# A fused RetNet attention and maxout FFN: plain first products for the first token tile, weight sums made one tile later

## The chip, the cores and the metric

The kernel runs on one core of one Trainium2 chip. The metric is the device time of one execution in microseconds (us). Five engines work side by side, each through its own instructions in order: TensorE (PE; the loading of its stationary operand is listed as PEld), VectorE (DVE), ScalarE (ACT), GpSimd (POOL), and SyncE (SP), whose queue issues nearly all transfers here.

## The reference

Causal attention with a decay (RetNet, parallel form) over 8 batches and 8 heads, then a feed-forward network that takes the maximum of three products:

```python
# q, k, v: (8, 8, 576, 64); w1, w2, w3: (512, 768); w_out: (768, 512)
scores = scale * np.matmul(q, k.transpose(0, 1, 3, 2))
gamma = 1.0 - 2.0 ** (-5.0 - np.arange(H, dtype=np.float32))
Dmat = np.where(rel >= 0, gamma[:, None, None] ** rel[None, :, :], 0.0)
attn = np.matmul(scores * Dmat[None], v).astype(np.float32)
x = attn.transpose(0, 2, 1, 3).reshape(B * S, H * D)          # (4608, 512)
h = np.maximum(np.maximum(x @ w1, x @ w2), x @ w3)
out = (h @ w_out).astype(np.float32)                          # (4608, 512)
```

The four weight matrices come as 64-bit floats and are brought to 32 bits in the kernel. All arithmetic is in 32-bit floats.

## The kernel before

The 4608 token rows are cut into 36 chunks of 128 rows (g) and 9 tiles of 512 rows (t), four chunks to a tile. Two things go on side by side: the attention of tile t + 1 and the FFN of tile t.

**Attention** of a chunk has three steps. `transposes` (L136) turns the decayed keys (`kd`, made on POOL in `decay_keys`, L130) and the queries on PE, and copies them out, kT on DVE and qT on ACT. `scores` (L149) makes the masked score block st and the running state (DVE L158, L169 or L171, POOL L172). `values` (L176) makes the output o and writes it to xT (L192); behind the last chunk of a tile DVE and POOL also make four sums of quarter blocks of xT (S, L197 to L200).

**The FFN** of a tile (`ffn`, L345) has nine units: a pair of 128-column blocks of the hidden layer (fp = 0, 1, 2) times one of the three weight matrices (i). A unit (`up`, L284) uses Strassen's scheme in Winograd's form: seven products of half-size blocks (two matmuls of 256 columns each, L293) in place of eight. It needs the S sums of xT and four sums of the weight quarters (L266, L267 on DVE; L269, L270 on POOL). Products are copied out by ACT (L298, L330) or added and compared on DVE (L311 to L333). Then four output blocks (`down`, L336) take six matmuls of 512 columns each, in one group per block (L339). In the trace each matmul of 32-bit floats shows as two instructions, so a count of x12 means six matmuls.

**Weights** come in 24 pieces of 128 x 512 (18 for the first products, 6 for the output), 512 KB each, with three buffers. `conversion` (L233) makes 32-bit floats of a piece from the two halves of its 64-bit words: `expo` and `frac` masks on DVE (L241, L246), three ACT passes (L242, L244, L248), `mant` on DVE (L249), the sign by ACT (L253), and two products on POOL, by the exponent (L254) and by the sign (L257). When both pieces of a pair are there, the four weight sums follow. The temporaries have two buffers.

**The order** is the order of the code. `convert(n)` puts n steps of the running conversion into the queues at that place. Attention's three steps alternate with units of the FFN (L388 to L397), and before, each of a unit's seven products was followed by `convert(2)` (L350), so conversions of later pieces stand in the queues of DVE, ACT and POOL between the evictions of earlier units.

## Time and profile before

| what | value |
|---|---|
| median of 3 runs | 928.27 us (927.96 to 930.12) |
| the profiled execution | 927.27 us, span 925.2 us |
| PE busy | 872.6 us (94%) |
| DVE, ACT, POOL busy | 387.5, 205.1, 177.8 us |
| granted clock of PE, mean | 0.989 |
| first matmul of the first unit, tile 0 | 43.91 us |
| first output block, tile 0 | 157.31 us |
| end of tile 0 | 183.08 us |
| tile 1 | 92.4 us |

"Busy" is the time in which an engine had at least one instruction running, and includes what an instruction waits once it has started. In a line of the trace the names are the program's with buffer numbers left out, out<-in; in square brackets stands the idle time before it and what ended it.

### The profile page before, as it was taken

The page shows a single profiled execution, that of the slowest core. Times are in us where ns is not written, and L with a number is a line of the kernel's source. Part 1 is how long each engine was busy: PE and PEld are TensorE (multiplying, and loading weights), DVE is VectorE, ACT ScalarE, POOL GpSimd, SP SyncE. Part 2 cuts the span into 40 slices and gives each one's busy share as a digit, 9 for nine tenths or more (in the row PEclk, how much of TensorE's full clock was granted, in tenths as well). Part 3 has the DMA queues.
Part 4 walks back from the last instruction along what each step waited for, and adds up shares of the span by engine and source line. Part 5 has one row for each costly group of instructions (what it writes and reads, how often), then busy time and mean ns, then how long its engine had stood idle before and what let it go on. Part 6 is the DMA issues. An engine that isn't in the chain of part 4 may idle for free.

```text
span 925.2 us, 11657 instructions
## 1 busy us (share of the span) xinstructions
PE 872.6 (94%) x4652; PEld 661.3 (71%) x4652; DVE 387.5 (42%) x692; ACT 205.1 (22%) x439; POOL 177.8 (19%) x154
## 2 busy tenths in 40 slices
PE   6676768999999999999999999999999999999998
PEld 5555555588758885888578857886788668866883
DVE  4887788244423442344334432433244334432330
ACT  2365555112111111211111111111111111111111
POOL 3767766110011001100111011100200020001000
PEclk9899999999999999999999999999999999999999
DMA  9525232150006000600060006000600050000001
GB/s 228 137 92 148 91 109 74 49 134 1 1 35 148 1 1 35 148 1 1 30 154 1 1 24 148 12 1 23 145 15 1 12 130 8 1 12 35 1 0 46
DMA packets 128550, 51.62 MB, mean 56 GB/s; under 512 B 113648, under 2 KB 122864, under 8 KB 128496
## 3 DMA queue, kind: packets, MB, share of 16 engines
q1 hardware_dynamic: 128064, 50.34, 20.6%
q8 instruction: 37, 0.61, 0.3%
q10 hardware_dynamic: 432, 0.53, 0.2%
q14 instruction: 17, 0.14, 0.0%
HBM read 41.42 MB, written 9.44 MB: 55 GB/s over the span
## 4 chain that ended last, share of the span: by engine, by line
PE 86%; DVE 7%; POOL 3%; ACT 2%; issue 1%; DMA 1%; SPq 0%; DVEq 0%; POOLq 0%; ACTq 0%
PE x L293 28%; PE down L339 20%; PE z L293 14%; PE y L293 7%; PE s L155 4%; PE o L185 3%; PE kv L166 3%; PE o L190 3%; PE kt L141 2%; DVE expo L241 2%; PE qt L141 2%; DVE mant L249 2%; POOL w L257 1%; POOL mant L254 1%; DVE frac L246 1%
## 5 line engine op out<-in xcount | busy, mean ns | idle before, releaser
L339 PE MATMUL down<-wout,h 128*128 128x512 f32 x432 | 189.9, 593 | 0.0
L293 PE MATMUL x<-S,T 128*128 128x256 f32 x648 | 169.3, 384 | 14.9 <-ACT u L298 9.3
L293 PEld LDWEIGHTS x<-S,T 128*128 128x128 f32 x648 | 123.0, 191 | 36.2 <-ACT u L298 12.4
L339 PEld LDWEIGHTS down<-wout,h 128*128 128x128 f32 x432 | 80.2, 190 | 91.8 <-issue 91.3
L172 POOL TENSOR_TENSOR state<-state,gs 128x512 f32<-128x512 f32 x24 | 31.1, 1296 | 388.4 <-DVE state L171 297.8
L293 PE MATMUL x<-S,w 128*128 128x256 f32 x324 | 85.6, 387 | 9.8 <-DVE h L321 7.2
L293 PE MATMUL z<-xT,T 128*128 128x256 f32 x324 | 84.6, 384 | 6.2 <-ACT p L298 5.8
L293 PE MATMUL z<-S,w 128*128 128x256 f32 x324 | 84.9, 385 | 0.0
L293 PE MATMUL x<-xT,w 128*128 128x256 f32 x324 | 84.9, 385 | 0.0
L293 PE MATMUL y<-xT,w 128*128 128x256 f32 x324 | 83.1, 379 | 0.0
L158 DVE TENSOR_TENSOR st<-s,causal 128x512 f32<-128x512 f32 x72 | 46.3, 685 | 78.7 <-PE s L155 78.7
L293 PEld LDWEIGHTS x<-S,w 128*128 128x128 f32 x324 | 56.5, 192 | 26.6 <-DVE h L321 5.1
L293 PEld LDWEIGHTS z<-xT,T 128*128 128x128 f32 x324 | 61.4, 191 | 16.8 <-POOL T L270 3.5
L298 ACT COPY p<-x 128x256 f32<-128x256 f32 x81 | 30.1, 371 | 187.2 <-PE x L293 187.2
L293 PEld LDWEIGHTS z<-S,w 128*128 128x128 f32 x324 | 62.7, 194 | 8.8
L293 PEld LDWEIGHTS y<-xT,w 128*128 128x128 f32 x324 | 61.6, 190 | 8.4
L321 DVE TENSOR_TENSOR tmp<-x,p 128x256 f32<-128x256 f32 x54 | 22.9, 424 | 104.8 <-PE x L293 104.1
L342 ACT COPY osb<-down 128x512 f32<-128x512 f32 x36 | 21.1, 585 | 200.1 <-PE down L339 200.1
L293 PEld LDWEIGHTS x<-xT,w 128*128 128x128 f32 x324 | 56.5, 192 | 6.3 <-issue 0.8
L130 POOL TENSOR_TENSOR kd<-kraw,gk 128x512 f32<-128x512 f32 x36 | 39.1, 1092 | 99.8 <-DMA kraw<-in_k_dram 84.8
L192 DVE TENSOR_TENSOR xT<-o,gq 128x512 f32<-128x512 f32 x36 | 24.8, 690 | 71.4 <-PE o L190 65.4
L298 ACT COPY u<-x 128x256 f32<-128x256 f32 x81 | 30.0, 370 | 100.8 <-PE x L293 99.4
(58 smaller groups left out, 924.8 us busy)
## 6 DMA issues: line engine op xcount, KB each, us to landing
bits<-in_moe_w_dram SPq DMA_DIRECT2D x18, 512.0 KB, 3.6
out_dram<-osb SPq DMA_DIRECT2D x36, 256.0 KB, 2.0
kraw<-in_k_dram SPq DMA_DIRECT2D x32, 256.0 KB, 4.0
qraw<-in_q_dram SPq DMA_DIRECT2D x32, 256.0 KB, 4.1
vraw<-in_v_dram SPq DMA_DIRECT2D x32, 256.0 KB, 4.1
bits<-in_moe_w_out_dram SPq DMA_DIRECT2D x6, 512.0 KB, 3.2
kraw<-in_k_dram SPq DMA_DIRECT2D x8, 128.0 KB, 3.5
qraw<-in_q_dram SPq DMA_DIRECT2D x8, 128.0 KB, 3.2
```

What stands on the lines that cost most here:

```text
L130: nc.gpsimd.tensor_tensor(t[:], raws.pop(("k", g))[:], gk[:].unsqueeze(2).to_broadcast([C, H, D]), op=ALU.mult)
L141: nc.tensor.transpose(pt[:, p, :], pair(src, p), ident[:C, :C])
L155: nc.tensor.matmul(s[j][:, p, :], lhsT=kT[r, p, :], rhs=qT[r, p, :], start=True, stop=True)
L158: nc.vector.tensor_tensor(st[:, j], s[j][:], masks[start_of(g)][:].unsqueeze(1).to_broadcast([C, NP, C]), op=ALU.mult)
L166: nc.tensor.matmul(kv[:, p, :], lhsT=pair(kd, p)[r:], rhs=pair(raws["v", g], p)[r:], start=True, stop=True)
L172: nc.gpsimd.tensor_tensor(t[:], t[:], gs[:], op=ALU.mult)
L185: nc.tensor.matmul(o[D * j:D * (j + 1), p, :], lhsT=vr[:, 2 * p + j, :], rhs=st[:, j, p, :], start=(p == 0), stop=(old == 0 and p == NP - ...
L190: nc.tensor.matmul(o[:, p, :old], lhsT=sd[:, p, :], rhs=qT[:, p, :old], start=False, stop=(p == NP - 1), skip_group_check=True)
L192: nc.vector.tensor_tensor(xT[t][:, :, i * C:(i + 1) * C], o[:], gq[:], op=ALU.mult)
L293: nc.tensor.matmul(out[:], lhsT=w[:, d * P:(d + 1) * P], rhs=xS[t][n][:, d, :], start=first and d == 0, stop=d == 1, skip_group_check=True)
L298: nc.scalar.copy(c[:], src[:])
L339: nc.tensor.matmul(ps[:], lhsT=h[:, fb, m * P:(m + 1) * P], rhs=w_sb["out", fb][:], start=(fb == 0), stop=(fb == NF - 1))
```

## The change

For tile 0 the first products are plain (`up_plain`): each of the 18 pieces gives one block of h by four matmuls of 512 columns into a whole PSUM bank of 512 columns; for matrix 0 ACT copies it to h, for matrices 1 and 2 DVE takes the maximum of h and it. Tile 0 so needs neither the S sums nor the weight sums. The weight sums are made by `weight_sums(n)`: the first two behind the third and fourth output block of tile 0, the others behind the units of tile 1, two units ahead of their use.

In the conversion the sign is no longer a factor. DVE takes the sign bit of the high word and puts it into the exponent factor (`bitwise_and`, then `bitwise_or`), and POOL multiplies once. A piece has four steps instead of five, and eight instructions instead of nine behind the load.

At the start the first weight piece is loaded behind chunk 2 and the second and third behind chunk 3; the key products and the first conversions stand at other places in the order.

```diff
--- before.py
+++ after.py
@@ -190,7 +190,7 @@
                 nc.tensor.matmul(o[:, p, :old], lhsT=sd[:, p, :], rhs=qT[:, p, :old],
                                  start=False, stop=(p == NP - 1), skip_group_check=True)
         nc.vector.tensor_tensor(xT[t][:, :, i * C:(i + 1) * C], o[:], gq[:], op=ALU.mult)
-        if i == CPT - 1:
+        if i == CPT - 1 and t > 0:
             x = xT[t]
             a11, a12, a21, a22 = (x[:, 2 * d:2 * d + 2, NH * r:NH * (r + 1)] for r in range(2) for d in range(2))
             s1, s2, s3, s4 = (spool.tile([P, 2, NH], FP32, tag=f"S{n}", name=f"S{n}") for n in (1, 2, 3, 4))
@@ -249,27 +249,26 @@
         nc.vector.scalar_tensor_tensor(out=mant[:], in0=frac[:], scalar=2.0 ** -20, in1=mant[:],
                                        op0=ALU.mult, op1=ALU.add)
         yield
-        sign = wtmp.tile([P, DM], FP32, tag="sign", name="sign")
-        nc.scalar.activation(sign[:], high, AF.Sign)
-        nc.gpsimd.tensor_tensor(mant[:], mant[:], expo[:].bitcast(FP32), op=ALU.mult)
-        yield
+        nc.vector.scalar_tensor_tensor(out=expo[:], in0=high, scalar=-2 ** 31, in1=expo[:],
+                                       op0=ALU.bitwise_and, op1=ALU.bitwise_or)
         w = w_sb[piece] = const.tile([P, DM], FP32, name=f"w{i}_{fb}")
-        nc.gpsimd.tensor_tensor(w[:], mant[:], sign[:], op=ALU.mult)
+        nc.gpsimd.tensor_tensor(w[:], mant[:], expo[:].bitcast(FP32), op=ALU.mult)
         load_weights(1)
         yield
-        if i == "out" or fb % 2 == 0:
+
+    def weight_sums(n):
+        if n >= len(units):
             return
+        fp, i = units[n]
         half = [slice(0, DM // 2), slice(DM // 2, DM)]
-        b11, b21 = (w_sb[i, fb - 1][:, r] for r in half)
-        b12, b22 = (w_sb[i, fb][:, r] for r in half)
-        t1, t2, t4 = (const.tile([P, DM // 2], FP32, name=f"T{n}_{i}_{fb}")[:] for n in (1, 2, 4))
+        b11, b21 = (w_sb[i, 2 * fp][:, r] for r in half)
+        b12, b22 = (w_sb[i, 2 * fp + 1][:, r] for r in half)
+        t1, t2, t4 = (const.tile([P, DM // 2], FP32, name=f"T{m}_{i}_{fp}")[:] for m in (1, 2, 4))
         nc.vector.tensor_tensor(t1, b12, b11, op=ALU.subtract)
         nc.vector.tensor_tensor(t2, b22, t1, op=ALU.subtract)
-        yield
         nc.gpsimd.tensor_tensor(b12, b22, b12, op=ALU.subtract)
         nc.gpsimd.tensor_tensor(t4, b21, t2, op=ALU.subtract)
-        wT[fb // 2, i] = {1: b11, 2: b21, 3: b22, 4: t4, 5: t1, 6: t2, 7: b12}
-        yield
+        wT[fp, i] = {1: b11, 2: b21, 3: b22, 4: t4, 5: t1, 6: t2, 7: b12}
 
     def convert_all():
         for piece in pieces:
@@ -342,15 +341,35 @@
         nc.scalar.copy(osb[:], ps[:])
         nc.sync.dma_start(out[t * NT + m * P:t * NT + (m + 1) * P, :], osb[:])
 
+    def up_plain(t, h, fb, i):
+        ps = (ps_x, ps_y)[fb % 2].tile([P, NT], FP32, tag="xy"[fb % 2], name="up")
+        for dc in range(NDC):
+            nc.tensor.matmul(ps[:], lhsT=w_sb[i, fb][:, dc * P:(dc + 1) * P], rhs=xT[t][:, dc, :],
+                             start=(dc == 0), stop=(dc == NDC - 1))
+        if i == 0:
+            nc.scalar.copy(h[:, fb, :], ps[:])
+        else:
+            nc.vector.tensor_tensor(h[:, fb, :], h[:, fb, :], ps[:], op=ALU.max)
+
     def ffn(t):
 
         h = hpool.tile([P, NF, NT], FP32, tag="h", name="h")
-        for fp, i in units:
-            for _ in up(t, h, fp, i):
-                convert(2)
+        for n, (fp, i) in enumerate(units):
+            if t == 0:
+                for fb in (2 * fp, 2 * fp + 1):
+                    up_plain(t, h, fb, i)
+                    convert(5 if n < 4 else 4)
+            else:
+                for _ in up(t, h, fp, i):
+                    pass
+                if t == 1:
+                    weight_sums(n + 2)
             yield
+        convert(4 * len(pieces))
         for m in range(NT // P):
             down(t, h, m)
+            if t == 0 and m >= 2:
+                weight_sums(m - 2)
             if m < NT // P - 2:
                 yield
         yield
@@ -358,39 +377,39 @@
 
     load(0)
     load(1)
-    load_weights(1)
     load(2)
     load_weights(1)
     load(3)
-    load_weights(1)
-    for g in range(3):
-        decay_keys(g)
+    load_weights(2)
+    decay_keys(0)
+    decay_keys(1)
     transposes(0)
     transposes(1)
+    decay_keys(2)
     scores(0)
-    decay_keys(3)
     transposes(2)
     values(0)
+    decay_keys(3)
     scores(1)
     convert(4)
     transposes(3)
     values(1)
     scores(2)
-    convert(6)
     load(4)
     values(2)
+    convert(2)
     scores(3)
-    convert(8)
     decay_keys(4)
+    convert(2)
     values(3)
+    convert(4)
     for t in range(N // NT):
         work = ffn(t)
         for g in range((t + 1) * CPT, (t + 2) * CPT):
             for step in (transposes, scores, values):
                 if g < NG:
-                    if step is transposes:
-                        if g + 1 < NG:
-                            load(g + 1)
+                    if step is transposes and g + 1 < NG:
+                        load(g + 1)
                     if step is scores and g + 1 < NG:
                         decay_keys(g + 1)
                     step(g)
```

What this does to the order, at three places. On POOL, ahead of the key product of chunk 4, with which tile 0's stage begins; before:

```order
L172 TENSOR_TENSOR state<-state,gs 128x512
L257 TENSOR_TENSOR w_0_318<-mant,sign 128x512
L254 TENSOR_TENSOR mant<-mant,expo 128x512
L257 TENSOR_TENSOR w_1_334<-mant,sign 128x512
L172 TENSOR_TENSOR state<-state,gs 128x512
L269 TENSOR_TENSOR w_1_334<-w_1_334 128x256
L270 TENSOR_TENSOR T_0_1_384<-w_0_318,T_0_1_383 128x256
L254 TENSOR_TENSOR mant<-mant,expo 128x512
L257 TENSOR_TENSOR w_0_401<-mant,sign 128x512
L130 TENSOR_TENSOR kd<-kraw,gk 128x512
L199 TENSOR_TENSOR S_427<-xT 128x512
L200 TENSOR_TENSOR S_428<-xT,S_426 128x512
```

and of the change:

```order
L172 TENSOR_TENSOR state<-state,gs 128x512
L255 TENSOR_TENSOR w_0_267<-mant,expo 128x512
L172 TENSOR_TENSOR state<-state,gs 128x512 x2
L130 TENSOR_TENSOR kd<-kraw,gk 128x512
L255 TENSOR_TENSOR w_1_376<-mant,expo 128x512
```

The key product now follows the two states directly; the second and third piece stand behind it, and the sums are gone from this place. On DVE, in the fourth unit of tile 0 before (T are weight sums, p and u kept products):

```order
L266 TENSOR_TENSOR T_1_3_707<-w_3_699,w_2_676 128x256
L267 TENSOR_TENSOR T_1_3_708<-w_3_699,T_1_3_707 128x256
L144 COPY kT<-kt 128x512
L241 TENSOR_SCALAR expo<-bits 128x512
L246 TENSOR_SCALAR frac<-bits 128x512
L311 TENSOR_TENSOR h<-y,p_737 128x256
L249 SCALAR_TENSOR_TENSOR mant<-frac,mant 128x512
L241 TENSOR_SCALAR expo<-bits 128x512
L246 TENSOR_SCALAR frac<-bits 128x512
L249 SCALAR_TENSOR_TENSOR mant<-frac,mant 128x512
L321 TENSOR_TENSOR h<-x,p_770 128x256
L324 TENSOR_TENSOR h<-z,u_757 128x256
```

and in the fourth and fifth of the change (L252 is the sign, L352 the maximum with a product; the first L352 here takes piece 8, and the last sign ahead of it is that of piece 12):

```order
L241 TENSOR_SCALAR expo<-bits 128x512
L246 TENSOR_SCALAR frac<-bits 128x512
L249 SCALAR_TENSOR_TENSOR mant<-frac,mant 128x512
L252 SCALAR_TENSOR_TENSOR expo<-bits,expo 128x512
L158 TENSOR_TENSOR st<-s_676,causal 128x512
L158 TENSOR_TENSOR st<-s_677,causal 128x512
L171 TENSOR_TENSOR state<-kv,state 128x512
L352 TENSOR_TENSOR h<-h,up 128x512
L241 TENSOR_SCALAR expo<-bits 128x512
L246 TENSOR_SCALAR frac<-bits 128x512
L249 SCALAR_TENSOR_TENSOR mant<-frac,mant 128x512
L252 SCALAR_TENSOR_TENSOR expo<-bits,expo 128x512
```

A unit has two evictions on DVE (none for matrix 0) instead of several of half the size, and each piece has four steps in a row. On POOL, behind the last conversion, the change has (w_1_376 and T_0_0 are of unit 0, w_1_445 and T_1_0 of unit 1, w_1_507 and T_2_0 of unit 2):

```order
L172 TENSOR_TENSOR state<-state,gs 128x512
L199 TENSOR_TENSOR S_1055<-xT 128x512
L200 TENSOR_TENSOR S_1056<-xT,S_1054 128x512
L269 TENSOR_TENSOR w_1_376<-w_1_376 128x256
L270 TENSOR_TENSOR T_0_0_1073<-w_0_267,T_0_0_1072 128x256
L269 TENSOR_TENSOR w_1_445<-w_1_445 128x256
L270 TENSOR_TENSOR T_1_0_1090<-w_0_404,T_1_0_1089 128x256
L269 TENSOR_TENSOR w_1_507<-w_1_507 128x256
L270 TENSOR_TENSOR T_2_0_1145<-w_0_465,T_2_0_1144 128x256
L130 TENSOR_TENSOR kd<-kraw,gk 128x512
```

where before two L199 and L200 were followed by the key products of the next chunks alone. The sums of the weights stand there now, ahead of the key product of a later chunk.

## The prediction

> **What bounds the kernel now.** First the busy times by stage. The stages are the start, the FFN's first products of tile 0 (43.69 to 157.31 us), its second products, and the whole tile 1. After the stretch stand span, PE, PEld, DVE, ACT and POOL busy, granted clock, DMA share and GB/s.
>
> ```profile
> core 0: us, PE busy (x) PEld busy (x) DVE busy (x) ACT busy (x) POOL busy (x), PEclk, DMA share, GB/s
> 43.69:157.31 113.62, 82.79 (x423) 63.88 (x423) 94.28 (x138) 65.43 (x116) 77.20 (x64) 0.93 0.36 105
> 157.31:183.08 25.77, 25.77 (x105) 13.39 (x105) 6.64 (x9) 2.93 (x5) 5.93 (x5) 1.00 0.08 31
> 183.08:275.50 92.42, 92.42 (x500) 70.40 (x499) 33.84 (x66) 15.26 (x37) 9.70 (x8) 1.00 0.18 46
> ```
>
> From 157.31 on PE is busy the whole time; nothing is to be had there but by less PE work. In tile 0's first products PE idles 113.62 - 82.79 = 30.8 us, and DVE (94.3) and POOL (77.2) together are busy for 171 us, so they overlap. Next the waits of that stretch, in total us, times and longest:
>
> ```profile
> PE x L293 <- ACT u L298: 9.3, 4, 3.4
> PE x L293 <- DVE h L321: 7.2, 3, 3.2
> ...
> DVE T L266 <- POOL w L257: 15.5, 7, 3.1
> ```
>
> PE waits for evictions that stand in the in-order queues of ACT and DVE behind conversions; those wait in turn, and DVE sits 15.5 us before the sums for the sign product of POOL. The timeline of DVE and POOL shows what sets the pace of these two:
>
> ```profile
> 75.40 0.42 DVE L241 TENSOR_SCALAR expo<-bits 128x512 int32<-128x512 int32 x1
> 75.63 1.33 POOL L254 TENSOR_TENSOR mant<-mant,expo 128x512 f32<-128x512 f32 x1 [1.23 <-DVE mant L249]
> ...
> 76.32 0.42 DVE L321 TENSOR_TENSOR tmp<-x,p 128x256 f32<-128x256 f32 x1 [0.50 <-ACT p L298]
> 76.66 0.58 DVE L246 TENSOR_SCALAR frac<-bits 128x512 int32<-128x512 int32 x1
> ...
> 77.03 1.33 POOL L257 TENSOR_TENSOR w<-mant,sign 128x512 f32<-128x512 f32 x1
> 77.34 1.57 DVE L249 SCALAR_TENSOR_TENSOR mant<-frac,mant 128x512 f32<-128x512 int32 x1
> ```
>
> A DVE operation between SBUF tiles that meets a running POOL product ends 0.28 to 0.55 us after that product does: frac ends at 77.24 (POOL 76.96), mant at 78.91 (POOL 78.36). An eviction from PSUM beside POOL keeps its 0.42. So conversion steps and POOL products exclude each other. One more view, the groups in this stretch (busy us, mean ns):
>
> ```profile
> L254 POOL TENSOR_TENSOR mant<-mant,expo 128x512 f32<-128x512 f32 x21 | 27.5, 1310 | 26.6 <-DVE mant L249 18.1 <-ACT expo L248 5.4 <-ACT sign L253 3.1
> L246 DVE TENSOR_SCALAR frac<-bits 128x512 int32<-128x512 int32 x21 | 21.1, 1003 | 0.0
> L249 DVE SCALAR_TENSOR_TENSOR mant<-frac,mant 128x512 f32<-128x512 int32 x21 | 20.1, 959 | 1.5
> L241 DVE TENSOR_SCALAR expo<-bits 128x512 int32<-128x512 int32 x20 | 19.1, 953 | 0.0
> L244 ACT ACTIVATE expo<-expo,top 128x512 f32<-128x512 int32 x21 | 15.2, 723 | 34.6 <-DVE expo L241 34.5
> L269 POOL TENSOR_TENSOR w<-w 128x256 f32<-128x256 f32 x8 | 7.7, 962 | 4.7 <-DVE T L266 4.7
> L270 POOL TENSOR_TENSOR T<-w,T 128x256 f32<-128x256 f32 x8 | 7.3, 912 | 0.0
> L266 DVE TENSOR_TENSOR T<-w,w 128x256 f32<-128x256 f32 x8 | 3.4, 423 | 15.5 <-POOL w L257 15.5
> L192 DVE TENSOR_TENSOR xT<-o,gq 128x512 f32<-128x512 f32 x8 | 5.5, 684 | 7.3 <-PE o L190 6.6 <-PE o L185 0.6
> ```
>
> Counting each step without its waiting, one unit of tile 0 (two pieces and their sums) needs of that shared resource 2 x (0.42 + 0.42 + 0.69 + 1.3 + 1.3) = 8.3 for conversions, 2 x 0.42 + 0.96 + 0.91 = 2.7 for sums, and at least 1 for the max between SBUF tiles and attention's POOL work: 12.0 us. The units take 12.6 (first start 43.91, end 157.31, nine units). The conversion pair bounds tile 0, not PE.
>
> **The change, start.** Before, PE waited for the key product of chunk 4, which stood on POOL behind the first sums and the third piece; DVE made S1 and S2 behind xT:
>
> ```profile
> 32.97 1.27 POOL L172 TENSOR_TENSOR state<-state,gs 128x512 f32<-128x512 f32 x1
> 33.12 1.16 PE L190 MATMUL o<-qT,state 128*128 128x128 f32 x8
> ...
> 37.76 0.68 DVE L192 TENSOR_TENSOR xT<-o,gq 128x512 f32<-128x512 f32 x1
> ...
> 40.60 1.49 POOL L130 TENSOR_TENSOR kd<-kraw,gk 128x512 f32<-128x512 f32 x1
> ...
> 42.14 1.11 PE L141 MATMUL kt<-ident,kd 128*128 128x128 f32 x4 [7.87 <-POOL kd L130]
> ...
> 43.91 1.62 PE L293 MATMUL x<-xT,w 128*128 128x256 f32 x4
> ```
>
> Now kd follows state directly (34.24), so transposes can begin near 35.5 instead of 42.14, and the first product near 36.4, 7.5 earlier. On DVE only two pieces stand ahead of the last xT: o ends at 34.28, xT at 35.0. The reordered loads take one weight piece (512 KB) from ahead of chunk 2's loads, and one from ahead of chunk 3's:
>
> ```profile
> 0.00:20.00 20.00, 11.60 (x88) 9.59 (x88) 6.36 (x13) 3.70 (x5) 5.20 (x14) 1.00 0.95 232
> 14.00 1.04 POOL L130 TENSOR_TENSOR kd<-kraw,gk 128x512 f32<-128x512 f32 x1 [4.02 <-DMA kraw<-in_k_dram]
> ```
>
> At 232 GB/s this is 524288 / 232000 = 2.3 us at most, at least 0 since DVE and PE follow closely; I take 1.5. DVE then turns to piece 2 at 33.5.
>
> **Tile 0's products on PE.** 72 matmuls of 512 columns replace 126 of 256. The rows from the chain of waits, where PE runs without a stop (x12 are six matmuls, x4 two):
>
> ```profile
> 157.31 5.15 PE down L339 x12
> 162.46 1.09 PE s L155 x16
> 163.55 1.09 PE kv L166 x8
> ...
> 169.79 1.02 PE o L185 x16
> 170.82 1.09 PE o L190 x8
> ...
> 183.95 0.86 PE y L293 x4
> ```
>
> And the two transposes' groups with the product behind them, from the timeline:
>
> ```profile
> 79.61 0.60 PE L141 MATMUL kt<-ident,kd 128*128 128x128 f32 x4
> ...
> 80.48 1.03 PE L293 MATMUL x<-xT,w 128*128 128x256 f32 x4
> ```
>
> Plain: 72 x 5.15 / 6 = 61.8 us; before: 63 x 0.86 = 54.2. PE gets 7.6 us more work. Three chunks of attention (1.09 + 1.09 + 1.02 + 1.09 = 4.3 each, and 80.48 - 79.61 = 0.87 for transposes) add 15.5: PE needs 77.3 us at least between the first product and the second products.
>
> **Conversions.** Per piece, ACT loses its sign pass and POOL one product of 1.3; DVE gains a step of the form of L249, two tensors in. Steps that meet no POOL product:
>
> ```profile
> 67.42 0.42 DVE L246 TENSOR_SCALAR frac<-bits 128x512 int32<-128x512 int32 x1
> ...
> 74.79 0.69 DVE L249 SCALAR_TENSOR_TENSOR mant<-frac,mant 128x512 f32<-128x512 int32 x1
> ```
>
> The trace has no bitwise step with two tensors. Its bounds are this 0.69 and the 1.57 of the held-up L249 at 77.34; I take 0.69 because POOL has then nothing of this piece to run: its one product waits for this very step. DVE's cycle for a piece is then: sign ends at 0; expo 0 to 0.42; POOL's product starts at 0.23 (75.63 against 75.40) and ends at 1.56; frac is held until 1.84; mant to 2.5; sign to 3.2. ACT's two steps, L244 and the like one behind it, take 0.72 each from expo's end and are through by 2.0, so they hide; where ACT waits for PE in a copy of h (units 0, 3 and 6), sign is late by that. So 3.2 us; the bounds are 2.2 (no hold-up: 0.42 + 0.42 + 0.69 + 0.69) and 3.9 (today's means: 0.95 + 1.00 + 0.96 + 0.96, with twice as much POOL work beside it).
>
> From piece 2 to piece 23 DVE's queue holds 22 pieces, 70.4 us; twelve max evictions and four kT, three xT, three state, six st copies, all of 128x512 from PSUM, 28 x 0.684 = 19.2; and POOL's attention work (four kd of 1.04 and two states of 1.27, 6.7) of which I count half, 3.4, as holding DVE up. Sum 93.0, so the last sign ends at 33.5 + 93.0 = 126.5. This is more than PE's 77.3, so DVE sets the end, by 10 us or so, since PE cannot start before 36.
>
> **The tail.** All six output pieces are flushed ahead of the second products. After the last sign come POOL's product (1.3) and the last matmul of the first output block (0.86): 128.7. Then s and kv 2.2, a block 5.15, o 2.1, two blocks 10.3, transposes 0.9: 149.3 is the start of tile 1, against 183.08. Gain 33.8.
>
> **Tile 1.** Nine sums of 2.7 us move here and into the last two blocks of tile 0, each two units ahead of its use. DVE is busy 33.8 of 92.4 there and POOL 9.7; the unit between, seven products of 0.86 and a third of a chunk's attention, hides them: nothing. If that cover were gone, seven sums would cost 7 x 2.7 = 18.9. The S tiles of tile 0 simply fall away.
>
> **A rule that speaks against it.** DVE is the busiest of the three helpers (94.28 against 65.43 and 77.20), and the sign goes to it. The Trainium skill (Perfetto Trace Analysis, "Optimizing Scalar/DVE Operations") advises the opposite, to offload a saturated DVE to ScalarE or even GpSimd, though it adds that DVE and GpSimd share an SBUF port, so that moves between these two may not help. The exclusion in the rows at 75 to 79 us agrees with that addition. By the advice the result would be the rival of the slow DVE below; by the rows each sign takes 0.69 where POOL's product took 1.3 of the same resource.
>
> **Rivals.** (1) *DVE stays slow*: today's held-up means persist, 3.9 instead of 3.2. For it: POOL still has a product per piece. Against it: half as many. 22 x 0.7 = 15 us later, gain 18.4, time 909.9. (2) *PE bound*: hold-ups fall under evictions, which POOL doesn't touch; about ten pieces are followed by one. Then tile 0's first products take 77.3 instead of 113.62 (36.3 less) and start 7.5 earlier: gain 43.8, time 884.5. Against it: the 93 us sum. (3) *Sums stall tile 1*, at POOL's and DVE's heads, because they queue behind that unit's last evictions: 33.8 - 18.9 = 14.9, time 913. Against it: a unit of slack. (4) *Conversion and products take turns*, the slower side. DVE's max eviction waits for PE, and every later conversion waits behind it. If it stood less than one piece behind what PE needs, a unit would take 2 x 3.2 + 2 x 3.43 + 1.7 = 15.0 instead of 12.6: nine units, 21.4 us more, less 7.5 for the start, 942. Against it: DVE's queue has two and a half to four whole pieces between a piece's sign and its eviction.
>
> **The numbers.** 927.27 for the profiled execution (span 925.2) less 33.8 is 893.5; the median lies 1.0 above that execution: 894.5. Chances: forecast 0.62 (886 to 904), slow DVE 0.13, PE bound 0.16, stalled sums 0.04, taking turns 0.05. The range 883 to 912 takes in PE's bound and the slow DVE and leaves out the last two and some of the edges. A difference under 0.3% (2.8 us) can't be told from none by a measurement of this kernel; of the cases only taking turns in part could land there. So faster 0.94, same 0.01, slower 0.05.
>
> **What would show it.** Tile 1's first product at 145 to 155 us; DVE busy above 90% between 40 and 125; sign steps near 0.69 and piece cycles near 3.2; PE's waits in that stretch on POOL's w, no longer on evictions; first output block held for the last wout; tile 1 still 92 to 93 us with PE at 100%. The forecast is wrong if PE waits in tile 1, if DVE idles at L352's evictions while PE waits for w, or if the sign steps exceed 1 us.

## The result, and the profile after

The changed kernel takes 888.66 us (median of 4 runs, 887.56 to 890.07) where the kernel before, run beside it, takes 928.12 (927.69 to 930.12): a ratio of 0.9572, with a 95% interval of 0.9551 to 0.9592. 39.5 us are gone; the prediction had 33.8. The profiled execution took 889.22 us, its span is 887.5. The head of its page:

```profile
PE 870.8 (98%) x4544; PEld 639.5 (72%) x4544; DVE 371.4 (42%) x681; ACT 185.8 (21%) x391; POOL 141.4 (16%) x128
...
PE   6999989999999999999999999999999999999998
```

PE is busy for 1.8 us less than before (872.6), yet the span is 37.7 us shorter: what went is idle time of PE, nearly all, and it went from the first slices. The same three stages, with the same columns, as in the prediction's first view, by the times of the new trace (first products of tile 0, its second products, tile 1):

```profile
35.20:112.53 77.33, 77.33 (x314) 40.19 (x313) 71.19 (x107) 45.78 (x69) 32.35 (x26) 1.00 0.59 171
112.53:145.89 33.36, 29.52 (x107) 15.42 (x106) 14.95 (x21) 6.37 (x10) 12.02 (x11) 0.90 0.11 35
145.89:238.30 92.41, 92.41 (x500) 69.95 (x499) 38.97 (x80) 15.28 (x37) 21.12 (x22) 1.00 0.18 46
```

The first products went from 113.62 us to 77.33, with PE busy in all of it. Before, PE idled 30.8 us there; its work was 77.33 less the 7.6 by which the plain products are longer, 69.7 at the pace of now, but PE was busy for 82.79, in short groups between waits and at a mean clock of 0.93. Thus 30.8 of idle time and 13.1 of slower running went and 7.6 of work came: 36.3. The second products went from 25.77 to 33.36 us, with 3.84 us idle and a clock of 0.90. Tile 1 takes 92.41 us against 92.42, though DVE has 5.1 and POOL 11.4 us more work in it. From tile 1's first product to the end of the span are 887.5 - 145.89 = 741.6 us, before 925.2 - 183.08 = 742.1. So the sums are free there, and everything happens ahead of tile 1, which starts 37.2 us earlier.

The second products are the one stage that lost. PE's timeline there (start, duration, operation, and in brackets the idle time ahead of it with its releaser):

```profile
112.53 3.60 PE L338 MATMUL down<-wout,h 128*128 128x512 f32 x8
117.24 1.12 PE L338 MATMUL down<-wout,h 128*128 128x512 f32 x2 [1.11 <-POOL wout L255]
121.10 2.07 PE L338 MATMUL down<-wout,h 128*128 128x512 f32 x2 [2.73 <-POOL wout L255]
123.10 2.08 PE L155 MATMUL s<-qT,kT 64*128 64x128 f32 x16
```

The first output block waits for the last two pieces of w_out. Behind the second wait the groups take about twice their time: two products took 0.86 and s 1.09 before. The first two parts of that stage, cut at 121.10 and 127.20, show the clock:

```profile
112.53:121.10 8.57, 4.73 (x13) 1.64 (x11) 6.15 (x10) 4.02 (x6) 3.38 (x4) 0.98 0.17 40
121.10:127.20 6.10, 6.10 (x27) 4.37 (x28) 1.29 (x2) 0.59 (x1) 0.94 (x1) 0.50 0.12 46
```

For 6.1 us after the second wait the granted clock is 0.50, half of full speed. Of the 33.36 - 25.77 = 7.6 us that the stage lost, 3.84 are waits; of the other 3.75, half of 6.1, 3.05, lies in this stretch. So 3.8 us of waits cost nearly twice their length.

DVE's conversions: the first step of piece 2, a piece with no eviction in it, and the sign of the last piece (timeline of DVE, with POOL's product between):

```profile
33.85 0.66 DVE L241 TENSOR_SCALAR expo<-bits 128x512 int32<-128x512 int32 x1
...
70.04 0.69 DVE L249 SCALAR_TENSOR_TENSOR mant<-frac,mant 128x512 f32<-128x512 int32 x1
70.65 0.68 DVE L252 SCALAR_TENSOR_TENSOR expo<-bits,expo 128x512 int32<-128x512 int32 x1
71.25 0.42 DVE L241 TENSOR_SCALAR expo<-bits 128x512 int32<-128x512 int32 x1
71.41 1.39 POOL L255 TENSOR_TENSOR w<-mant,expo 128x512 f32<-128x512 f32 x1 [1.76 <-DVE expo L252]
71.58 1.50 DVE L246 TENSOR_SCALAR frac<-bits 128x512 int32<-128x512 int32 x1
...
73.80 0.69 DVE L252 SCALAR_TENSOR_TENSOR expo<-bits,expo 128x512 int32<-128x512 int32 x1
...
119.01 0.69 DVE L252 SCALAR_TENSOR_TENSOR expo<-bits,expo 128x512 int32<-128x512 int32 x1 [0.41 <-ACT expo L248]
```

From sign to sign are 3.15 us, of which frac takes 1.5, held by POOL's product (it ends 0.28 after that one). The 22 pieces and their 28 evictions take from 33.85 to 119.70, 85.85 us; the prediction had 93.0. Their groups in that stretch (busy us, mean ns, idle ahead):

```profile
L246 DVE TENSOR_SCALAR frac<-bits 128x512 int32<-128x512 int32 x22 | 21.6, 983 | 0.0
L249 DVE SCALAR_TENSOR_TENSOR mant<-frac,mant 128x512 f32<-128x512 int32 x22 | 15.2, 692 | 2.8 <-ACT mant L242 0.8
L252 DVE SCALAR_TENSOR_TENSOR expo<-bits,expo 128x512 int32<-128x512 int32 x22 | 15.1, 688 | 4.4 <-ACT expo L248 4.4
L352 DVE TENSOR_TENSOR h<-h,up 128x512 f32<-128x512 f32 x12 | 8.2, 680 | 0.0
```

The sign step (L252) takes 0.688, as the step it was priced by. DVE never waits for PE at the max evictions (L352).

### The profile page after: what moved, and what is told of

It reads as the page before. It is cut to its first block, busy times and chain, and to the rows that moved or that the text cites. A ratio compares the mean times of both kernels' runs of the same rounds, so it can differ in the third digit from the quotient of the medians.

```text
span 887.5 us, 11310 instructions
## 1 busy us (share of the span) xinstructions
PE 870.8 (98%) x4544; PEld 639.5 (72%) x4544; DVE 371.4 (42%) x681; ACT 185.8 (21%) x391; POOL 141.4 (16%) x128
## 4 chain that ended last, share of the span: by engine, by line
PE 87%; DVE 5%; ACT 3%; issue 2%; POOL 1%; DMA 1%; SPq 0%; DVEq 0%; POOLq 0%; ACTq 0%
PE x L292 28%; PE down L338 21%; PE z L292 14%; PE y L292 7%; PE s L155 4%; PE o L185 3%; PE kv L166 3%; PE o L190 3%; PE kt L141 2%; PE qt L141 2%; ACT expo L244 1%; ACT expo L248 1%; DVE expo L241 1%; DVE expo L252 1%; DVE h L352 1%
## 5 line engine op out<-in xcount | busy, mean ns | idle before, releaser
L292 PE MATMUL x<-S,T 128*128 128x256 f32 x576 | 147.8, 379 | 0.0
L292 PEld LDWEIGHTS x<-S,T 128*128 128x128 f32 x576 | 109.2, 190 | 15.1
L292 PE MATMUL x<-xT,w 128*128 128x256 f32 x288 | 74.9, 382 | 0.0
L292 PE MATMUL x<-S,w 128*128 128x256 f32 x288 | 74.3, 380 | 0.0
L292 PE MATMUL z<-xT,T 128*128 128x256 f32 x288 | 73.9, 379 | 0.0
L292 PE MATMUL z<-S,w 128*128 128x256 f32 x288 | 73.9, 379 | 0.0
L292 PE MATMUL y<-xT,w 128*128 128x256 f32 x288 | 73.9, 379 | 0.0
L347 PE MATMUL up<-xT,w 128*128 128x512 f32 x144 | 63.4, 593 | 0.0
L292 PEld LDWEIGHTS z<-S,w 128*128 128x128 f32 x288 | 54.7, 190 | 7.4
L292 PEld LDWEIGHTS z<-xT,T 128*128 128x128 f32 x288 | 54.1, 189 | 8.1
```

The lines of the kernel that those rows point to most:

```text
L292: nc.tensor.matmul(out[:], lhsT=w[:, d * P:(d + 1) * P], rhs=xS[t][n][:, d, :], start=first and d == 0, stop=d == 1, skip_group_check=True)
L347: nc.tensor.matmul(ps[:], lhsT=w_sb[i, fb][:, dc * P:(dc + 1) * P], rhs=xT[t][:, dc, :], start=(dc == 0), stop=(dc == NDC - 1))
```

## The experiments

Two theories came from the prediction. *DVE sets the end of tile 0*: its queue, with the steps that POOL's product holds up, ends at 119.70, and the second products follow from there. The rival was *PE sets it*: PE runs from 35.20 to 112.53 without a wait, exactly the 77.3 us that the prediction gave as its least, so an earlier DVE would bring only the 7.6 us of the stage behind. Two more questions were what each part of the change is worth, and whether shared (exclusive) work of DVE and POOL had set the pace before. Times stand beside the kernel before, which ran next to them (928.2 to 929.5 us); "the change" means the changed kernel's 888.66 us.

**The start as before.** Loads, decay products and conversions are issued in the old order; the conversion steps that are given out there are 12, three whole pieces as before.

```diff
+    load_weights(1)
     load(2)
...
-    load_weights(2)
-    decay_keys(0)
-    decay_keys(1)
+    load_weights(1)
+    for g in range(3):
+        decay_keys(g)
...
-    convert(4)
+    convert(3)
...
+    convert(5)
     load(4)
     values(2)
-    convert(2)
     scores(3)
+    convert(4)
     decay_keys(4)
-    convert(2)
     values(3)
-    convert(4)
```

> The first part undone: loads, key products and first conversions stand where they stood before, the rest is as changed. Theory (VectorE's conversion queue sets the end of tile 0's stage, so only its start counts): piece 2's first step stays near 34 to 35 us, the last sign ends about 1 us later than 119.7, time 889 to 892. Rival (every us by which PE starts earlier is a us of gain): PE's first plain product comes 3 to 7 us later, and the time is 892 to 896.

Measured: 895.11 us (894.8 to 896.81), ratio 0.9644 [0.9628, 0.966], 6.5 us more than the change. PE's first product starts at 40.84 instead of 35.21, 5.6 us later, and tile 1 starts 5.8 us later (151.53 against 145.73, both in PE's timeline). So the later start counts nearly in full. In between two things nearly cancel: the first pair of products is longer by 1.7 us at a granted clock of 0.52 (40.84 to 44.00), and behind the same waits for w_out the clock is low for only 3.6 us, not 6.1. DVE, whose queue was to be the bound, had time to lose, as the timelines of PE, ACT and DVE show:

```profile
40.84 8.73 PE L347 MATMUL up<-xT,w 128*128 128x512 f32 x16
...
46.18 0.58 ACT L350 COPY h<-up 128x512 f32<-128x512 f32 x1 [4.55 <-PE up L347]
...
47.45 0.69 DVE L249 SCALAR_TENSOR_TENSOR mant<-frac,mant 128x512 f32<-128x512 int32 x1 [5.49 <-ACT mant L242]
```

DVE's mant step waits 5.49 us for ACT's pass over the bits, which stands in ACT's queue behind the copy of the first product, which waits 4.55 us for PE. So the two theories are not apart: DVE's queue is tied to PE's first product through ACT's order, and a late PE makes DVE late by about as much. The prediction had the same link in one clause (a sign is late where ACT waits in a copy of h), without a price for the first unit.

**One more product on POOL.** Each piece's product is made twice, once into a scratch tile.

```diff
+        extra = wtmp.tile([P, DM], FP32, tag="extra", name="extra")
+        nc.gpsimd.tensor_tensor(extra[:], mant[:], expo[:].bitcast(FP32), op=ALU.mult)
```

> The changed kernel with POOL's product of each piece made twice, the first time into a scratch tile; nothing waits for that one but POOL. Theory (conversion steps on VectorE and POOL products exclude each other): VectorE's loop for a piece grows by most of 1.27 us, from about 3.15 to 4.2, the last sign ends 20 us later, time 905 to 915. Rival (POOL, busy 40% there, has room): the last weight is 1.3 us later and nothing else, time 889 to 892.

Measured: 903.53 us (2 runs), ratio 0.9731 [0.971, 0.9752], 14.9 us more than the change, or 0.68 a piece, and 1.5 us below the theory's range. The groups of DVE in tile 0:

```profile
L246 DVE TENSOR_SCALAR frac<-bits 128x512 int32<-128x512 int32 x22 | 31.8, 1447 | 0.0
L249 DVE SCALAR_TENSOR_TENSOR mant<-frac,mant 128x512 f32<-128x512 int32 x22 | 24.5, 1114 | 2.1
```

POOL's own load is not what costs: it is DVE's two steps, 464 and 422 ns longer than in the change (983 and 692). For 22 pieces that is 19.5 us; but DVE now waits for ACT less (idle time ahead of L249 and L252 2.1 us instead of 7.2), and the last sign ends at 133.88, 14.2 us later than in the change. DVE steps between SBUF tiles and POOL products do exclude each other.

**POOL's product on DVE.** The product of a piece is made by DVE, between mant and sign of the next piece.

```diff
+    def finish():
+        if pending:
+            w, mant, expo = pending.pop()
+            nc.vector.tensor_tensor(w[:], mant[:], expo[:].bitcast(FP32), op=ALU.mult)
...
                                        op0=ALU.mult, op1=ALU.add)
+        finish()
         yield
...
-        nc.gpsimd.tensor_tensor(w[:], mant[:], expo[:].bitcast(FP32), op=ALU.mult)
+        pending.append((w, mant, expo))
```

> The changed kernel with POOL's product made on VectorE, between mant and sign of the next piece. VectorE gets 24 steps of 0.69 more and POOL none. Theory (exclusion): frac is no longer held up (1.1 us a piece) and a step of 0.6 comes in, so the loop of a piece shrinks from 3.15 to about 2.7, the last product ends near 112, PE no longer waits in the first output block: 7 us less, time 880 to 884. Rival (VectorE is bound by the number of its own steps): 22 x 0.6 = 13 us later, time 900 to 903.

Measured: 886.48 us (885.71 to 888.49), ratio 0.9545 [0.9527, 0.9562], 2.2 us less than the change, a third of what was expected; the two intervals overlap. The loop did what the theory says. PE's first pair of products, steps of one piece on DVE, and two later places on DVE:

```profile
35.66 8.83 PE L356 MATMUL up<-xT,w 128*128 128x512 f32 x16
...
72.09 0.68 DVE L260 SCALAR_TENSOR_TENSOR expo<-bits,expo 128x512 int32<-128x512 int32 x1
72.69 0.41 DVE L248 TENSOR_SCALAR expo<-bits 128x512 int32<-128x512 int32 x1
73.03 0.41 DVE L253 TENSOR_SCALAR frac<-bits 128x512 int32<-128x512 int32 x1
...
74.76 0.68 DVE L260 SCALAR_TENSOR_TENSOR expo<-bits,expo 128x512 int32<-128x512 int32 x1
...
110.67 0.69 DVE L361 TENSOR_TENSOR h<-h,up 128x512 f32<-128x512 f32 x1 [1.27 <-PE up L356]
...
121.45 0.69 DVE L238 TENSOR_TENSOR wout<-mant,expo 128x512 f32<-128x512 f32 x1
```

With a step more, DVE's cycle is 2.67 us (72.09 to 74.76) instead of 3.15. But DVE now catches up with PE, waits for it at an eviction at 110.67, and the last pieces stand behind such evictions: the last product ends at 122.1, where in the change PE could go on at 121.10. Part of the expected gain went there, to the order of the last pieces. Another part went at the start: PE's first pair begins at 35.66 and takes 8.75 us where the change's takes 6.96 from 35.21, so that the first products end 2.2 us later (114.77 against 112.53). PE waits for no weight in that pair; its granted clock is 0.61 from 35.66 to 40.00, behind a wait of 1.60 us for POOL's kd. In the change the clock stayed at 1.00 behind a wait of 1.59; why the two differ stays open. The group of frac in tile 0 shows that nothing holds its 22 steps any more:

```profile
L253 DVE TENSOR_SCALAR frac<-bits 128x512 int32<-128x512 int32 x22 | 9.2, 418 | 0.0
```

**That product on DVE, with the pieces ahead of the evictions.** As the kernel just told, with the first two pieces' product left on POOL, and five conversion steps after each first product throughout, so that no piece is left behind the last evictions.

```diff
+        if piece in pieces[:2]:
+            nc.gpsimd.tensor_tensor(w[:], mant[:], expo[:].bitcast(FP32), op=ALU.mult)
+        else:
+            pending.append((w, mant, expo))
...
-                    convert(5 if n < 4 else 4)
+                    convert(5)
```

> The product on VectorE from the third piece on (the first two stay on POOL, so that PE's first two products are not late), and five conversion steps behind every product instead of four from the fifth unit on, so that only half a piece is left behind the last unit's products. Theory (without POOL beside it a piece costs VectorE 2.67 us, and what kept the run with the product on VectorE at 886 was the late second piece and three pieces queued behind evictions that wait for PE): PE has no wait of over 1 us between the first product and tile 1, time 880 to 884. Rival (the last weights are late whatever the order): 885 to 888.

Measured: 882.69 us (881.6 to 883.3), ratio 0.9511 [0.9495, 0.9527], 6.0 less than the change. PE's only wait between 34 and 160 us, and then the window from its first transposes to tile 1 (which starts at 139.04):

```profile
PE kt L141 <- POOL kd L130: 1.6, 1, 1.6
```

```profile
35.00:140.00 105.00, 104.98 (x429) 55.43 (x430) 88.02 (x149) 55.34 (x80) 16.26 (x14) 1.00 0.48 139
```

PE waits once, ahead of its first product, and runs at full clock from there on: this is the PE-bound case of the prediction's second rival, priced there at 884.5. Two things are different from that kernel at once, and what each brought was not separated. The late second piece that the expectation names is not what the trace of the kernel just told shows: that piece was ready at 37.67, inside the first product.

**Two output blocks side by side.** Nothing in the conversions is changed. In tile 0 the first five of six products of output blocks 0 and 1 are made before the sixth of block 0, and the sixth of block 1 follows the scores, so that PE has work while the last piece is converted (`down_part` makes some of a block's six products, and copies the block out behind the sixth).

```diff
...
+        if t == 0:
+            ps = [ps_y.tile([P, DM], FP32, tag="y", name="down") for m in range(2)]
+            for m in range(2):
+                down_part(t, h, m, ps[m], range(NF - 1))
+            down_part(t, h, 0, ps[0], [NF - 1])
         for m in range(NT // P):
-            down(t, h, m)
+            if t == 0 and m == 1:
+                down_part(t, h, 1, ps[1], [NF - 1])
+            elif t > 0 or m > 1:
+                down(t, h, m)
```

> The changed kernel with tile 0's first two output blocks interleaved: five of six matmuls of both go ahead of the sixth of the first, so 4.3 us of PE work stand between the fifth weight and the last. Theory (the tail loses 3.84 us by waiting for the last weights, and 3.75 by the low granted clock that follows the wait): both vanish, tile 1 starts at 138 to 139 instead of 145.9, time 880 to 883. Rival (the low clock is independent of the wait): only the wait goes, time 884 to 886.

Measured: 883.28 us (882.41 to 883.72), ratio 0.9512 [0.9498, 0.9526], 5.4 less than the change and 0.3 above the theory's range. PE's only wait between 34 and 160 us, and then most of the stage of the second products:

```profile
PE down L346 <- POOL wout L255: 1.1, 1, 1.1
```

```profile
112.50:139.00 26.50, 25.41 (x104) 13.06 (x103) 14.04 (x20) 6.37 (x10) 11.24 (x11) 1.00 0.11 36
```

One wait of 1.1 is left, the clock stays at 1.00, and the stage takes 27.1 us (111.75 to 138.88, the window above begins a little inside it) instead of 33.2 (112.53 to 145.73 in the same view). The clock's loss went with the wait that it followed. Together with the run before it this says that tile 0 has two bounds within a few us of each other: a faster DVE and a PE that has other work meanwhile give the same time, and beyond it PE's own work is left.

**The sign as before.** Sign again by a pass on ACT and a second POOL product, in four steps a piece.

```diff
-        nc.vector.scalar_tensor_tensor(out=expo[:], in0=high, scalar=-2 ** 31, in1=expo[:],
-                                       op0=ALU.bitwise_and, op1=ALU.bitwise_or)
+        sign = wtmp.tile([P, DM], FP32, tag="sign", name="sign")
+        nc.scalar.activation(sign[:], high, AF.Sign)
+        nc.gpsimd.tensor_tensor(mant[:], mant[:], expo[:].bitcast(FP32), op=ALU.mult)
...
-        nc.gpsimd.tensor_tensor(w[:], mant[:], expo[:].bitcast(FP32), op=ALU.mult)
+        nc.gpsimd.tensor_tensor(w[:], mant[:], sign[:], op=ALU.mult)
```

> The sign's move undone, plain products and start as changed: ACT makes the sign, POOL makes two products a piece, VectorE has one step less. The run with POOL's product made twice cost 15 us (0.7 us a piece); here VectorE also loses a step of 0.6 a piece. Theory (only the sum of exclusive work and VectorE's own work counts): the two nearly cancel, POOL's second product is +15 and the lost step -13, ACT has 2.9 us a piece and stays hidden: time 888 to 898. Rival (the sign's move is a main source of the gain): 903 to 912.

Measured: 891.71 us (890.73 to 892.84), ratio 0.9614 [0.9596, 0.9632], 3.05 more than the change by the medians. The groups of DVE in tile 0:

```profile
L246 DVE TENSOR_SCALAR frac<-bits 128x512 int32<-128x512 int32 x22 | 30.8, 1400 | 0.0
L249 DVE SCALAR_TENSOR_TENSOR mant<-frac,mant 128x512 f32<-128x512 int32 x22 | 23.7, 1076 | 2.1
```

frac takes 1400 ns instead of 983 and mant 1076 instead of 692, so the step of 688 ns that DVE is spared is more than used up by 801 ns of hold-up; PE waits 5.9 us for w_out instead of 3.8. The profiled executions differ by less than the medians: tile 1 starts at 146.55 against 145.73, both read in PE's timeline (the 145.89 above is where the chain that ended last has it).

**The plain products undone.** The units of tile 0 are made from seven products with their evictions, and the sums are made in tile 0, as before; sign and start are as in the change. A piece has a step fewer than before, so 12 conversion steps go to a unit, not 14.

```diff
-        for n, (fp, i) in enumerate(units):
-            if t == 0:
-                for fb in (2 * fp, 2 * fp + 1):
-                    up_plain(t, h, fb, i)
-                    convert(5 if n < 4 else 4)
...
+        for fp, i in units:
+            for n, _ in enumerate(up(t, h, fp, i)):
+                convert(2 if n < 6 else 0)
```

> The plain products undone: tile 0 uses seven half-size products a unit again, with S sums and weight sums in tile 0; sign on VectorE and the start's order as changed. Theory (the sums and the many evictions in tile 0 are most of what was saved): a unit takes 11.0 to 11.7 us instead of 8.6, time 905 to 915. Rival (sign and start bring most): 893 to 899.

Measured: 924.45 us (922.98 to 927.4), ratio 0.9967 [0.995, 0.9983]: 3 to 4 us less than the kernel before, and neither theory's number. Counted as in the prediction, a unit needs 2 x (0.42 + 0.42 + 0.69 + 0.69 + 1.3) + 2.7 + 1.0 = 10.7 us of what DVE and POOL share, 1.3 less than before; but its nine units take from 34.81 to 152.70, 13.1 us each, where they took 12.6. Part of that is the count: PE's first unit starts 9.1 us earlier than before, but the last ends only 4.6 earlier. The start and the end of the units, the waits of PE (in total us, times, longest), and the place around 71 us:

```profile
34.81 1.03 PE L291 MATMUL x<-xT,w 128*128 128x256 f32 x4
...
152.70 5.32 PE L337 MATMUL down<-wout,h 128*128 128x512 f32 x12
```

```profile
PE x L291 <- ACT u L296: 13.1, 8, 3.2
PE x L291 <- DVE tmp L319: 4.8, 4, 2.8
PE x L291 <- DVE h L319: 4.7, 2, 2.8
PE x L291 <- ACT p L296: 4.6, 1, 4.6
PE z L291 <- ACT p L296: 2.6, 1, 2.6
```

```profile
68.87 1.27 POOL L255 TENSOR_TENSOR w<-mant,expo 128x512 f32<-128x512 f32 x1 [5.02 <-DVE expo L252]
...
70.17 0.43 DVE L264 TENSOR_TENSOR T<-w,w 128x256 f32<-128x256 f32 x1 [1.05 <-POOL w L255]
...
70.97 0.95 DVE L241 TENSOR_SCALAR expo<-bits 128x512 int32<-128x512 int32 x1
...
71.95 0.72 ACT L244 ACTIVATE expo<-expo,top 128x512 f32<-128x512 int32 x1 [2.12 <-DVE expo L241]
72.58 0.35 ACT L296 COPY p<-z 128x256 f32<-128x256 f32 x1
...
73.08 1.10 PE L291 MATMUL z<-xT,T 128*128 128x256 f32 x4 [2.59 <-ACT p L296]
```

A sum on DVE waits for POOL's product, the next piece's expo waits behind that sum, ACT waits for expo, the copy of a product that PE needs for its next one stands behind that on ACT, and PE waits 2.59 us for the copy. By the order of the queues, PE's late products then hold up the evictions, and these the conversions. These waits are 29.8 us, about the 30.8 that PE idled before, and of the same kind as those shown there (for u 9.3, for h 7.2). So turns are taken within a unit here, and with the half-size products, taking work from DVE and POOL moves tile 0 by less than that work. A plain product has one eviction behind its four matmuls, and PE's next product doesn't wait for it (no such wait from 35.20 to 112.53 in the change).

**The plain products and the later sums alone.** Sign and start as before, in the edits shown above for each.

> Of the change only the plain products with the weight sums in tile 1; sign by ACT and POOL and the order of the start are as before. Theory (parts add: the sign's move brought 3 us and the start 6.5): 888.7 + 3.0 + 6.5 = 898, at most 901. Rival (the three parts need each other): 904 or more.

Measured: 899.87 us (898.82 to 900.6), ratio 0.9682 [0.9664, 0.97]: 29.6 us less than the kernel before. This is three quarters of the change, and what start (6.5) and sign (3.05) add, seen from the other end, makes the sum: 39.2 of 39.5 us. With the plain products the parts add up.

**The sign on DVE alone.** The kernel before with nothing but the new sign step; five steps a piece and 14 to a unit, as before.

```diff
-        sign = wtmp.tile([P, DM], FP32, tag="sign", name="sign")
-        nc.scalar.activation(sign[:], high, AF.Sign)
-        nc.gpsimd.tensor_tensor(mant[:], mant[:], expo[:].bitcast(FP32), op=ALU.mult)
+        nc.vector.scalar_tensor_tensor(out=expo[:], in0=high, scalar=-2 ** 31, in1=expo[:],
+                                       op0=ALU.bitwise_and, op1=ALU.bitwise_or)
         yield
...
-        nc.gpsimd.tensor_tensor(w[:], mant[:], sign[:], op=ALU.mult)
+        nc.gpsimd.tensor_tensor(w[:], mant[:], expo[:].bitcast(FP32), op=ALU.mult)
```

> Of the change only the sign on VectorE; tile 0 has its half-size products, its sums and the start as before. Theory (in tile 0 as before VectorE is the engine that ends last, busy or held up for 83% of the time; the run with sign and start changed was at 924.5, and the start is worth 4 to 7): 926 to 933, no gain, though exclusive work falls by 0.6 us a piece. Rival (exclusive work sets the pace, as the prediction had it): 24 x 0.6 = 14 us less, 912 to 917.

Measured: 921.55 us (920.26 to 922.57), ratio 0.9915 [0.9897, 0.9934], 7.9 less than the kernel before, between the two theories. The profiled executions differ by 4.7 (922.57 against 927.27). The units' start and end:

```profile
43.31 1.92 PE L292 MATMUL x<-xT,w 128*128 128x256 f32 x4
...
152.83 5.32 PE L338 MATMUL down<-wout,h 128*128 128x512 f32 x12
```

The units take 12.2 us; 1.3 us less shared work a unit brought 0.4. The kernel that has the new start besides begins its units at 34.81 and ends them at 152.70, nearly at the same time: with half-size products PE's earlier start brings nothing there, for PE waits in the units instead. By the medians that kernel gains less (3 to 4 us), by the profiled executions about as much (922.98 us). The two also differ in the conversion steps given to a unit (14 and 12), which was not tried apart.

**The sums in tile 0.** Three of a unit's four sums are made in tile 0, behind the second piece; the fourth, which overwrites a weight that the plain product reads, stays in tile 1.

```diff
+        nc.vector.tensor_tensor(t1, b12, b11, op=ALU.subtract)
+        nc.vector.tensor_tensor(t2, b22, t1, op=ALU.subtract)
+        yield
+        nc.gpsimd.tensor_tensor(t4, b21, t2, op=ALU.subtract)
...
-                    convert(5 if n < 4 else 4)
+                    convert(6 if n < 4 else 5)
```

> The changed kernel with three of the four weight sums of each pair (two on VectorE, one on POOL) made in tile 0 between the conversions, as before, and only the fourth (on POOL) in tile 1. Theory (exclusive work in tile 0 is the price): nine times 2 x 0.42 + 0.91 = 15.8 us, somewhat less where evictions lie above POOL: time 898 to 905. Rival (POOL and VectorE absorb them since PE is the bound at 77 us): 889 to 891.

Measured: 903.81 us (903.42 to 904.07), ratio 0.974 [0.9724, 0.9755], 15.2 more than the change. PE waits in tile 0:

```profile
PE s L155 <- DVE kT L144: 7.0, 2, 4.1
PE down L343 <- POOL wout L255: 6.6, 4, 2.6
```

With the plain products the sum of the shared work does set the time: three sums a unit, 0.42 + 0.42 + 0.91 = 1.75, nine times, are 15.8. So putting three of a unit's four sums where DVE and POOL idle is worth about 15 us by itself.

**The key product of chunk 4 ahead.** The kernel with the product on DVE and the pieces ahead, and `decay_keys(4)` moved ahead of `scores(3)`, against PE's last wait.

```diff
+    decay_keys(4)
     scores(3)
-    decay_keys(4)
     convert(2)
```

> The kernel of the run e8_dve_and_ahead with the key product of chunk 4 moved ahead of the scores of chunk 3, so that it stands on POOL ahead of the last state product. Theory (from the first plain product on PE never waits, so what it starts earlier is gained in full): transposes no longer wait 1.6 us for POOL, the first product follows the last xT, 1.2 us less, time 881 to 882. Rival (the last xT or the load of chunk 4 is the bound there): no difference, 882.5 to 883.

Measured: 882.51 us (5 runs, 882.29 to 882.94), ratio 0.9497 [0.9481, 0.9513]; beside the kernel without it (0.9511 [0.9495, 0.9527]) no difference can be told. The wait changed its name:

```profile
35.28 7.13 PE L359 MATMUL up<-xT,w 128*128 128x512 f32 x16 [0.43 <-DVE xT L192]
```

The first product waits for xT and starts at 35.28; without the move it started at 35.95, and 0.7 us can't be told apart here. Three versions stand at 882.5 to 883.3 us, faster than both kernels: 4.9 to 5.0% below the kernel before and 0.6 to 0.7% below the change.

## Why the prediction was right, and where not

**Direction and time.** 894.5 was forecast and 888.66 measured, inside the likeliest case (886 to 904). Tile 1 starts at 145.89, forecast 149.3. The difference, 3.4 us, is made of three terms, two of them large and of opposite sign, so that the time is nearer than its parts, and that is luck: DVE begins piece 2 at 33.85 instead of 33.5 (+0.35), its queue takes 85.85 instead of 93.0 (-7.15), and the tail behind the last sign takes 26.2 instead of 22.8 (+3.4). The other 2.4 us of the 5.8 lie in the rest of the span (0.5), in what lies around it (1.7 instead of 2.1), and in the profiled execution's place among the runs (0.6 above their median, where 1.0 below was assumed).

**The step that was mis-sized: DVE's queue of 93.0.** From start to start of DVE's instructions between 33.85 and 119.70, the 22 pieces take 69.1 us with 5.2 of waiting for ACT in it, 3.14 each; the forecast had 3.2 and was right there (-1.3), in part by luck: expo and frac are held up less (668 and 983 ns, together 1.65, where it counted 1.84), and 0.24 a piece of waiting for ACT came in, which it had as hidden. The 28 evictions take 16.7, 0.60 each, not 0.684 (-2.5): the rows list 0.68, but neighbours start 0.60 apart, as the steps mant, sign and expo do at 70.04, 70.65 and 71.25. And the 3.4 for POOL's attention work did not appear as a term of its own (-3.4).

**The step that was missed: the tail's clock.** Waits of the first output block for w_out were expected, and the block was placed rightly behind the last sign. That PE would then run at a clock of 0.50 for 6.1 us was not in the sum; 3.05 us of the stage's loss lie in that stretch, and the run with paired blocks shows that they go with the wait.

**DVE or PE.** The forecast put DVE 10 us or so behind PE and gave PE's bound 0.16. PE's 77.3 us were exact, 77.33, without any wait; DVE's last sign came 7.2 us behind them (119.70 against 112.53), and 3.84 us of this became waits of PE in the second products. So the forecast's mechanism held by a margin smaller than its error, and the second rival (884.5) is what the versions at 882.5 to 883.3 are.

**What bound the kernel before.** "The conversion pair bounds tile 0, not PE" was right in its parts, but not the only limit. That the pair exclude each other is shown by both product runs (15 us for an extra POOL product; a cycle of 2.67 instead of 3.15 without any). But 12.0 of 12.6 us a unit was near agreement and no proof: with 10.7 a unit took 13.1 and 12.2. The chain that ended last, followed through the nine units, runs in the kernel before for 60 of 113.4 us on DVE, 18 on POOL, 12 on ACT and only 14 on PE; with the sign on DVE alone it has 52, 5, 9 and 37 of 109.5; with the plain products undone 59, 6, 14 and 28 of 117.9. So conversions and sums did hold most of it, and what left POOL came back in large part as PE's products: the fourth rival's taking of turns stood close behind, in the kernel before. How much of the gain of the plain products is due to it, and how much to the sums that left tile 0 with them (15.2), no run separates fully. In the change it does not occur, for the reason given against it: DVE never idles at L352.

**The sign.** 0.69 a step was right (0.688), and the trade paid: 3.05 us in the change, 7.9 alone (by the medians; 1.5 and 4.7 by the profiled executions). The rule weighed in the prediction, to offload a saturated DVE (the Trainium skill, Perfetto Trace Analysis, "Optimizing Scalar/DVE Operations"), would have had the opposite sign. Its addition has two halves. That DVE and GpSimd share an SBUF port fits the rows (frac takes 1.50 us beside a POOL product). That moves between the two might not help is not what these runs show for the direction to DVE: the sign's move helped, since a POOL product holds DVE up by 0.80 us a piece, more than the step of 0.69 that replaces it. Moving the other product too shortened DVE's cycle to 2.67 us, but by itself brought only 2.2 us, with overlapping intervals.

**Sums and start.** Tile 1 hides the sums (92.41 against 92.42 us, PE at 100%), so the third rival fell; in tile 0 they would cost 15.2. The first product started at 35.21, forecast 36.4; undoing the new start costs 6.5 us, near the 7.5 that the PE-bound rival put on it, since DVE's queue follows PE's first product.

**The signs listed** came as written but for one: tile 1 at 145.89, sign steps of 0.688, PE's waits on w_out only, the first output block held. DVE is busy for 78.69 of the 85.85 us of its queue (92%), but for 73.35 of the 85 us from 40 to 125 (86%, not above 90), since its queue ended at 119.70.

## What to carry to other kernels

When two engines' work adds up to nearly the time of a stage, take a part of it away in thought and ask which wait would still stand: here, with 11.7 us less of shared work, waits of PE for small copies in the queues of ACT and DVE left the stage only 4 us shorter (109.5 us instead of 113.4), and fewer, larger products with one late eviction each removed them at the price of 7.6 us more PE work. Work with slack of a whole tile (the sums) belongs where its engines idle. And a wait of a few us on PE can cost nearly as much again in clock behind it (3.05 us behind 3.84 in the change), so it pays to keep PE fed with work that is ready, as the paired output blocks do.

## What the runs showed of the hardware

DVE instructions listed with 0.68 us start 0.60 apart when they follow each other, and those listed with 0.41 or 0.42 are followed 0.33 to 0.34 later (71.25 to 71.58 in the change; 72.69 to 73.03 with the product on DVE). A bitwise step with two tensors, one of them every other word of the 64-bit input, takes 0.688 us at 128x512, as the arithmetic step does. Behind PE's waits of 1.11 and 2.73 us within 8.6 us the granted clock was 0.50 for 6.1 us; behind nearly the same two waits (1.04 and 2.73) in the run with the old start it was 0.54 for 3.6 us; behind a single wait of 2.15 us, with the product on DVE, 0.58 for 3.0 us; and behind a single wait of 1.1 us it stayed at 1.00 with the paired blocks. So the length of a wait alone does not say what it costs in clock. A max eviction from PSUM keeps its 0.68 where SBUF steps are held by POOL to 1.50.
